# New places in the hand-laid order of a linear-attention and mixture-of-attention kernel: the first six chunks, the turning of x, and all the rest

## The chip, the cores and the metric

The kernel runs on one core of one Trainium2 chip. The metric is device time in microseconds (us), from the start of the program to its end. Time before: 364.91 us, the median of three runs (364.50 to 365.39).

## What is computed

Two layers, one behind the other, in float32.

```python
# layer 1, per batch b (4), head h (8), time t (768), head size 48
y[t]  = r[t] @ (state + outer(u * k[t], v[t]))
state = w[:, None] * state + outer(k[t], v[t])
# x = the heads of y side by side: 4 x 768 x 384
# layer 2, a mixture of 4 attentions; each token keeps its 2 best by the gate
logits = x @ w_gate
for e in range(4):
    q, k, v = x @ wq[e], x @ wk[e], x @ wv[e]          # 768 x 64 each
    a = softmax(causal(q @ k.T / 8))
    out += gate_weight[:, e:e+1] * (a @ v @ wo[e])      # weight 0 where e isn't kept
```

## The kernel before

**Chunks and groups.** Layer 1 runs in 24 chunks of 128 tokens (n = 0 to 23, six to a batch). Layer 2 runs in 8 groups of three chunks (G = 0 to 7, two to a batch): g = G % 2 is 0 for the first half of a batch and 1 for the second, which looks back at twice as many keys.

**A chunk** goes through these steps. `load_chunk` (L107, L108) and `load_vh` (L114) bring k, r and v by DMAs from the SP queue. `a_decay` (L279, L281) multiplies k and r by tables of powers of w, on VectorE (DVE) for the first three chunks and on GpSimd (POOL) after that. `a_ku` (L288, L290) runs on POOL. `a_transpose` turns k and r on TensorE (PE, L309), and ScalarE (ACT) copies them out (L315, L321). `a_state` (PE, L367) and `a_scores` (PE, L329) are issued together as a burst; `a_sum` (DVE, L378) and `a_put` (ACT, L388) take the state out, `a_mask` (two DVE instructions, L335) the scores. `a_out` (PE, L347) makes the outputs. `a_own` (two DVE instructions, L297 and L299) and `a_add` (DVE, L351) finish x, `a_clear` (POOL, L356) zeroes a buffer again. `a_xt` turns x on PE (L398) and copies the rounded high part out on ACT (L401); `a_xl` takes the low part on DVE (L408). For the first six chunks the second copies of v are not loaded again but copied on ACT (`load_zv`, four instructions at L128, and `copy_vh`, L119); later chunks load them by DMA (L130, L116).

**A group** goes through `m_proj` (keys and queries, PE L440; then ACT L450 and L455, DVE L452 and L457, and the DMA `tq<-xq` at L462), `m_values` (PE L473), `m_gate` (small DVE instructions), `m_scores` (PE L523 and L524, DVE L530, ACT L532), `m_weigh` (DVE L538 and L539, POOL L545), `m_turn` (PE L553, ACT L556), `m_av` (PE L570, ACT L576, DVE L577) and `m_out` (PE L586 to L588, ACT L590, store L592).

**Weights.** Each weight is loaded and split into a high and a low half: `load_qk`, `load_v`, `load_o` (SP), `hi_*` (ACT: L243, L256, L266), `lo_*` (DVE: L246, L259, L269).

**PSUM.** Every PE step but `m_scores` takes one of four buffers `ps`; `m_scores` takes one of two `psb`.

**What sets the order.** At the end of the kernel every step is put into a list with a place, a number in units of one group; the numbers in the dictionary `ORDER` are the offsets of the places. The list is sorted, and the steps are traced in that order. The framework's scheduler then lays each engine's queue by that order, and may let a step go ahead whose inputs its own time model holds ready while an earlier one is not; on the chip each queue runs strictly in the order laid. So a place is a priority, not a time. For a chunk the base is t = (n - 6) / 3 (plus `late` for chunks 3 to 5), and for a group's projection G - 1. Chunk n's burst stands at t + burst + slot[n % 6], its `a_out` just ahead of the burst of chunk n + 1.

Of the kernel before, what the change touches and what calls it, by code (L numbers as in the profile page):

```python
# [13 lines left out]
PSUM = bass.MemoryType.PSUM  # L14

ORDER = {
    "copy_vh": -0.4344, "xl": 0.0307, "own_step": 0.015, "add": 0.0416, "sum": 0.028, "mask": 0.1351, "clear":
    0.025, "weigh": 0.2685, "put": 0.2094, "load": -0.764, "decay": -0.4403, "late": 0.0203, "early": 0.1635,
    "early_project": -0.0474, "copy_zv": -0.5015, "load_uw": -0.4719, "load_vh": -0.5697, "load_zv": 0.0993,
    "transpose": -0.2131, "own": -0.3686, "burst": -0.0849, "xt": 0.376, "project": 0.1529, "project_step":  # L20
    0.0403, "attend": [-0.389, -0.3286], "av": [0.3013, 0.1265, 0.0118], "slot": [-0.0706, 0.0091, 0.0451,
    -0.0689, 0.0077, -0.0758], "mix": [0.4071, 0.6088], "mix_step": 0.0598, "load_qk": -0.8926, "load_v":
    0.3849, "load_o": 0.17, "attend_step": -0.0463, "values": 0.1812, "tail": 0.059, "tail_step": 1.2167,
}
FIRST = """
"""
# [12 lines left out]
def decay_attention_then_mixture_of_attention(  # L39
# [21 lines left out]
    NC = S // C  # L61
# [7 lines left out]
    GC = 3  # L69
# [203 lines left out]
    xt = {}  # L273
# [388 lines left out]
    def at(time, f, *args):  # L662
        steps.append((time, len(steps), f, args))

    for n in range(B * NC):
        t = (n - 2 * GC) / GC + (ORDER["late"] if GC <= n < 2 * GC else 0)
        at(t + ORDER["load"], load_chunk, n)
        at(t + ORDER["decay"], a_decay, n, 0)
        at(t + ORDER["decay"], a_decay, n, 1)
        at(t + ORDER["load_vh"], load_vh, n)  # L670
        at(t + ORDER["copy_zv" if n < EARLY_V else "load_zv"], load_zv, n)
        if n < EARLY_V:
            at(t + ORDER["copy_vh"], copy_vh, n)
        at(t + ORDER["transpose"], a_transpose, n)
        at(t + ORDER["own"], a_ku, n)

        at(t + ORDER["burst"] + 1 / GC + ORDER["slot"][(n + 1) % NC], a_out, n)
        at(t + ORDER["burst"] + 1 / GC + ORDER["slot"][(n + 1) % NC] + ORDER["own_step"], a_own, n)
        at(t + ORDER["burst"] + 1 / GC + ORDER["slot"][(n + 1) % NC] + ORDER["add"], a_add, n)
        if n + NL < B * NC:  # L680
            at(t + ORDER["burst"] + 1 / GC + ORDER["slot"][(n + 1) % NC] + ORDER["clear"], a_clear, n)
        t += ORDER["slot"][n % NC]
        at(t + ORDER["burst"] + 0.001, a_state, n)
        at(t + ORDER["burst"] + ORDER["sum"], a_sum, n)
        at(t + ORDER["burst"] + ORDER["put"], a_put, n)
        at(t + ORDER["burst"] + 0.003, a_scores, n)
        at(t + ORDER["burst"] + ORDER["mask"], a_mask, n)
        at(t + ORDER["xt"], a_xt, n)
        at(t + ORDER["xt"] + ORDER["xl"], a_xl, n)
    for G in range(NGR):  # L690
        g = G % NG
        nk = (g + 1) * GC
        t = G - 1 + ORDER["project"] - (0 if G else ORDER["early_project"])
# [6 lines left out]
        for e in range(E):  # L700
            t = G + e / E - (0 if G else ORDER["early"])
            if G == NGR - 1:
                t = G - ORDER["tail"] + e / E * ORDER["tail_step"]
# [88 lines left out]
```

## Time and profile before

| what | value |
|---|---|
| median of three runs | 364.91 us |
| the profiled execution's own time | 365.44 us |
| its span, first to last instruction | 363.7 us |
| busy in the span: PE, ACT, DVE, POOL | 94%, 72%, 63%, 54% |
| DMA, all 16 engines | 39.01 MB, mean 107 GB/s |

The profile is of one execution. Engines run at the same time; a share is busy time over the span. A wait in brackets, as `[1.20 <-DVE rabuf L335]`, is idle time of the engine just before the row and what ended it. Line numbers are those of the kernel before.

### The profile page before, as it was taken

How to read it: one execution, taken by the hardware profiler on the slowest of the kernel's cores; microseconds unless marked ns; L12 is line 12 of the kernel's file. 1: busy time of each engine (PE TensorE's matmuls, PEld its weight loads, DVE VectorE, ACT ScalarE, POOL GpSimd, SP SyncE). 2: the span in 40 equal slices, each digit the busy share in tenths (PEclk: the TensorE clock that was granted, in tenths of full speed). 3: DMA queues.
4: the chain of work that ended last, by engine and by line, in shares of the span. 5: the costliest groups of instructions: out<-in, count | busy, mean ns of one | idle time of the engine just before them, and what ended most of it. 6: DMA issues, size and time to landing. Idle time of an engine off the chain costs nothing.

```text
span 363.7 us, 10097 instructions
## 1 busy us (share of the span) xinstructions
PE 341.3 (94%) x3764; PEld 297.1 (82%) x3764; DVE 229.5 (63%) x645; ACT 261.2 (72%) x646; POOL 194.7 (54%) x272
## 2 busy tenths in 40 slices
PE   6877898999999999999999999999999999999995
PEld 2667787888899886999898896999898886998763
DVE  4897477778856565578667555478667554565400
ACT  7889667857885766757794857758795856778851
POOL 5389636856876267456776267465935053113520
PEclk9898999999999999999999999999999999999998
DMA  8994588484546945186637546196413410161101
GB/s 136 211 161 75 105 176 167 89 174 107 108 84 149 190 78 100 41 177 136 136 70 163 146 82 119 29 193 135 104 31 88 110 43 2 30 168 45 43 23 65
DMA packets 118484, 39.01 MB, mean 107 GB/s; under 512 B 111010, under 2 KB 114340, under 8 KB 118436
## 3 DMA queue, kind: packets, MB, share of 16 engines
q1 hardware_dynamic: 118436, 38.37, 52.0%
q8 instruction: 30, 0.49, 0.6%
q14 instruction: 18, 0.15, 0.1%
HBM read 21.05 MB, written 4.72 MB: 71 GB/s over the span
## 4 chain that ended last, share of the span: by engine, by line
PE 70%; DVE 9%; ACT 9%; DMA 4%; issue 4%; POOL 2%; SPq 1%; ACTq 0%; DVEq 0%; POOLq 0%
PE ps L440 11%; PE ps L570 11%; PE ps L553 8%; PE ps L473 7%; PE psb L523 5%; PE ps L347 5%; PE psb L524 5%; PE ps L309 5%; PE ps L586 3%; PE ps L367 2%; DMA tq<-xq 2%; PE ps L329 2%; PE ps L587 2%; PE ps L588 2%; DVE rabuf L335 2%
## 5 line engine op out<-in xcount | busy, mean ns | idle before, releaser
L545 POOL TENSOR_SCALAR pr<-pr,f,gate 128x128 f32<-128x128 f32 (+5 forms) x96 | 67.5, 716 | 84.0 <-DVE f L539 43.1
L530 DVE CUSTOM_DVE_ANT_0 pr<-psb,after 128x384 f32<-128x384 f32 (+5 forms) x96 | 58.8, 620 | 31.2 <-PE ps L553 20.0
L556 ACT ACTIVATE pt<-ps 128x384 f32<-128x384 f32 x144 | 55.7, 421 | 17.7 <-PE ps L553 15.7
L532 ACT ACTIVATE pr<-pr,nm 128x384 f32<-128x384 f32 (+5 forms) x96 | 64.2, 670 | 2.7 <-DVE nm L530 1.6
L553 PE MATMUL ps<-ident,pr 128*128 128x128 f32 x336 | 56.9, 278 | 1.2 <-ACT pt L556 0.9
L523 PE MATMUL psb<-tk,tq 128*128 128x384 f32 (+1 forms) x144 | 48.7, 341 | 3.8 <-DVE nm L530 2.3
L388 ACT ACTIVATE zvbuf<-z 64x384 f32<-64x384 f32 x48 | 25.1, 522 | 32.7 <-DVE z L378 28.3
L570 PE MATMUL ps<-pt,vv 128*64 128x384 f32 (+2 forms) x288 | 43.5, 422 | 0.3 <-ACT pt L556 0.3
L553 PEld LDWEIGHTS ps<-ident,pr 128*128 128x128 f32 x336 | 38.7, 141 | 6.0 <-ACT pt L556 1.8
L524 PE MATMUL psb<-tk,tq 128*128 128x384 f32 (+1 forms) x144 | 42.3, 312 | 0.0
L281 POOL TENSOR_TENSOR kdbuf<-kdbuf,tab_k 128x384 f32<-128x384 f32 x21 | 21.4, 1020 | 38.1 <-DMA kdbuf<-in_k_dram 29.9
L570 PEld LDWEIGHTS ps<-pt,vv 128*64 128x64 f32 x288 | 20.6, 137 | 20.9 <-issue 16.4
L335 DVE TENSOR_TENSOR rabuf<-ps,before 64x512 f32<-64x512 f32 x48 | 33.0, 688 | 1.9 <-PE ps L329 0.8
L440 PE MATMUL ps<-xt_hi,wqk_hi 128*128 128x384 f32 x96 | 33.9, 354 | 0.0
L440 PE MATMUL ps<-xt_hi,wqk_lo 128*128 128x384 f32 x96 | 32.3, 337 | 0.0
L440 PE MATMUL ps<-xt_lo,wqk_hi 128*128 128x384 f32 x96 | 32.3, 336 | 0.0
L523 PEld LDWEIGHTS psb<-tk,tq 128*128 128x128 f32 x144 | 27.2, 189 | 6.3 <-DVE nm L530 3.6
L347 PE MATMUL ps<-zvbuf,rabuf 128*64 128x48 f32 x768 | 29.6, 228 | 2.8 <-DVE rabuf L335 1.5
L347 PEld LDWEIGHTS ps<-zvbuf,rabuf 128*64 128x64 f32 x768 | 26.4, 141 | 6.7 <-ACT zvbuf L388 1.7
L329 PE MATMUL ps<-rabuf,kt 128*64 128x64 f32 x768 | 28.6, 224 | 1.5 <-DVE xq L457 1.0
L452 DVE TENSOR_TENSOR tk<-ps,tk 64x384 fp32r<-64x384 f32 x32 | 17.8, 555 | 19.3 <-ACT tk L450 18.6
L321 ACT ACTIVATE rabuf<-ps 64x512 f32<-64x512 f32 x48 | 28.2, 588 | 1.9 <-PE ps L309 1.6
(113 smaller groups left out, 782.8 us busy)
## 6 DMA issues: line engine op xcount, KB each, us to landing
tq<-xq SPq DMA_DIRECT2D x64, 192.0 KB, 3.5
kdbuf<-in_k_dram SPq DMA_DIRECT2D x24, 192.0 KB, 3.8
rdbuf<-in_r_dram SPq DMA_DIRECT2D x24, 192.0 KB, 3.6
vhbuf<-in_v_dram SPq DMA_DIRECT2D x24, 192.0 KB, 3.5
out_dram<-o SPq DMA_DIRECT2D x23, 192.0 KB, 2.0
zvbuf<-in_v_dram SPq DMA_DIRECT2D x72, 48.0 KB, 3.0
vhbuf<-in_v_dram SPq DMA_DIRECT2D x18, 96.0 KB, 3.3
pr<-in_moe_wk_dram SPq DMA_DIRECT2D x3, 128.0 KB, 3.9
```

Of the source, the lines that this page charges most:

```text
L329: nc.tensor.matmul(ps[rows, i, p, :], kt[:, p, half], ra[:, par, i, p, :], start=True, stop=True)
L335: nc.vector.tensor_tensor(ra[rows, par].rearrange("s i p t -> s (i p) t"), ps[rows].rearrange("s i p t -> s (i p) t"), before[rows, None, ...
L347: nc.tensor.matmul(ps[half, 2 * p + par, :], ra[:, par, i, p, :], zv[:, par, i, p, :], start=True, stop=True)
L440: nc.tensor.matmul(ps, a[:, t, m0:m0 + P], x[:, t, :], start=i == 0, stop=i == n - 1)
L523: nc.tensor.matmul(o, tq[e][:, 0, q], tk[:, e, :n], start=True, stop=False)
L524: nc.tensor.matmul(o, tq[e][:, 1, q], tk[:, e, :n], start=False, stop=True)
L530: nc.vector.tensor_tensor_reduce(pr[:, :N], ps, after[:, S - N:], 1.0, 3e38, op0=OP.add, op1=OP.min, accum_out=nm)
L532: nc.scalar.activation(pr[:, :N], pr[:, :N], AF.Exp, bias=nm, scale=-1.0, accum_out=sums[:, e, j, 0:1])
L545: nc.gpsimd.tensor_scalar(p[:, :N], p[:, :N], f[:, i], gate[:, i, e:e + 1], op0=OP.mult, op1=OP.mult)
L553: nc.tensor.transpose(pst[:, j, :], mg[G]["p", e, j][:, i * C:(i + 1) * C], ident)
L556: nc.scalar.activation(pt[:, j0:], pst[:, j0:], AF.Copy)
L570: nc.tensor.matmul(psy[par * HD:par * HD + HD, j0 * C:], vv[:, i % GC, e, :], mg[G]["t", e, i][:, j0:].rearrange("s j t -> s (j t)"), star ...
```

## The change

Five things are changed, all in the list of places; no instruction is added or removed. (1) Bursts of chunks 0 to 5 take their offset from a new list, `slot_first`; those of chunks 6 to 23 from `slot`. (2) `a_xt` and `a_xl` of chunk n are placed from the place of its `a_out` (by `xt_first` for chunks 0 to 5, by `xt` after that), and no longer from its burst. (3) `a_mask`, `a_sum`, `a_put`, `a_state`, `a_scores` keep their form. (4) All other numbers are new. (5) The rest of the code is rewritten to the same meaning.

```diff
 ORDER = {
-    "copy_vh": -0.4344, "xl": 0.0307, "own_step": 0.015, "add": 0.0416, "sum": 0.028, "mask": 0.1351, "clear":
-    0.025, "weigh": 0.2685, "put": 0.2094, "load": -0.764, "decay": -0.4403, "late": 0.0203, "early": 0.1635,
-    "early_project": -0.0474, "copy_zv": -0.5015, "load_uw": -0.4719, "load_vh": -0.5697, "load_zv": 0.0993,
-    "transpose": -0.2131, "own": -0.3686, "burst": -0.0849, "xt": 0.376, "project": 0.1529, "project_step":
-    0.0403, "attend": [-0.389, -0.3286], "av": [0.3013, 0.1265, 0.0118], "slot": [-0.0706, 0.0091, 0.0451,
-    -0.0689, 0.0077, -0.0758], "mix": [0.4071, 0.6088], "mix_step": 0.0598, "load_qk": -0.8926, "load_v":
-    0.3849, "load_o": 0.17, "attend_step": -0.0463, "values": 0.1812, "tail": 0.059, "tail_step": 1.2167,
+    "slot_first": [-0.0343, 0.0357, 0.066, -0.1135, -0.0011, -0.0651], "xt_first": 0.1508, "copy_vh": -0.3641,
+    "xl": 0.0089, "own_step": 0.0212, "add": 0.0461, "sum": 0.0171, "mask": 0.0441, "clear": 0.1139, "weigh":
+    0.347, "put": 0.1258, "load": -0.7169, "decay": -0.7152, "late": 0.0256, "early": 0.2341, "early_project":
+    -0.0171, "copy_zv": -0.4341, "load_uw": -0.4254, "load_vh": -0.4969, "load_zv": 0.0179, "transpose":
+    -0.2194, "own": -0.3837, "burst": -0.0773, "xt": 0.0468, "project": 0.1693, "project_step": 0.0363,
+    "attend": [-0.3869, -0.4547], "av": [0.3045, 0.1347, 0.0193], "slot": [0.0302, 0.0103, 0.0887, 0.012,
+    -0.0119, -0.0758], "mix": [0.4039, 0.5741], "mix_step": 0.0739, "load_qk": -0.8591, "load_v": 0.17,
+    "load_o": -0.0251, "attend_step": -0.0373, "values": 0.1807, "tail": 0.0527, "tail_step": 1.507,
 }
...
-        at(t + ORDER["burst"] + 1 / GC + ORDER["slot"][(n + 1) % NC], a_out, n)
...
-        t += ORDER["slot"][n % NC]
-        at(t + ORDER["burst"] + 0.001, a_state, n)
...
-        at(t + ORDER["xt"], a_xt, n)
-        at(t + ORDER["xt"] + ORDER["xl"], a_xl, n)
+        mine, next_one = (ORDER["slot_first"][x] if x < NC else ORDER["slot"][x % NC] for x in (n, n + 1))
+        t_out = t + ORDER["burst"] + 1 / GC + next_one
+        at(t_out, a_out, n)
...
+        at(t_out + ORDER["xt_first" if n < NC else "xt"], a_xt, n)
+        at(t_out + ORDER["xt_first" if n < NC else "xt"] + ORDER["xl"], a_xl, n)
+        t += ORDER["burst"] + mine
+        at(t + 0.001, a_state, n)
...
```

## Rows read from the trace of the kernel before

**Rows 1.** The page's first part: the span, then busy time, share and instructions of each engine.

```profile
span 363.7 us, 10097 instructions
PE 341.3 (94%) x3764; PEld 297.1 (82%) x3764; DVE 229.5 (63%) x645; ACT 261.2 (72%) x646; POOL 194.7 (54%) x272
```

**Rows 2.** Busy time of each engine by stage: the stretch in us, its length, then busy us (instructions) of PE, PE's weight loads, DVE, ACT, POOL, then PE's granted clock, the DMA share and GB/s.

```profile
0.00:9.50 9.50, 6.44 (x20) 2.47 (x20) 4.37 (x24) 7.12 (x13) 5.27 (x21) 1.00 0.85 139
9.50:37.00 27.50, 21.37 (x339) 18.77 (x339) 23.38 (x38) 24.44 (x54) 19.51 (x24) 0.88 0.95 145
37.00:50.00 13.00, 11.21 (x130) 10.46 (x130) 7.49 (x15) 7.28 (x17) 6.88 (x10) 1.00 0.72 141
50.00:100.00 50.00, 46.95 (x634) 42.59 (x632) 38.87 (x118) 36.83 (x93) 33.71 (x47) 1.00 0.66 131
100.00:345.00 245.00, 240.90 (x2559) 213.29 (x2561) 154.32 (x451) 178.84 (x455) 126.74 (x169) 1.00 0.46 100
345.00:364.00 19.00, 14.41 (x90) 9.53 (x86) 1.11 (x2) 6.71 (x18) 2.59 (x3) 0.93 0.11 42
```

**Rows 3.** The same for PE alone around the end of the third chunk: busy us, granted clock, DMA share, GB/s.

```profile
26.00:30.00 4.00, 2.02 (x31) 1.00 0.94 140
30.00:34.00 4.00, 3.21 (x54) 0.57 0.26 50
```

**Rows 4.** The chain of work that ended last, from 27 to 49 us: start, length, what.

```profile
27.25 0.34 DVE wv_lo L259
...
28.06 1.15 DVE wv_lo L259
...
29.24 0.69 DVE rabuf L335
...
29.97 0.69 DVE rabuf L335
...
41.16 0.49 ACT tk L450
...
42.25 0.57 DVE xq L457
...
43.43 4.93 DMA tq<-xq
```

**Rows 5.** PE in order of time at the start: start, length, what, and in brackets the idle time before it.

```profile
28.20 0.52 PE L398 MATMUL ps<-ident,ownv 128*128 128x128 f32 x3 [1.58 <-DVE ownv L351]
...
30.79 1.95 PE L347 MATMUL ps<-zvbuf,rabuf 128*64 128x48 f32 x32 [1.20 <-DVE rabuf L335]
...
40.07 1.14 PE L347 MATMUL ps<-zvbuf,rabuf 128*64 128x48 f32 x32
...
42.87 1.15 PE L329 MATMUL ps<-rabuf,kt 128*64 128x64 f32 x32 [0.98 <-DVE xq L457]
...
48.49 0.41 PE L523 MATMUL psb<-tk,tq 128*128 128x384 f32 x1 [0.81 <-DMA tq<-xq]
```

**Rows 6.** ACT in order of time, 39 to 41 us, same columns.

```profile
39.11 1.48 ACT L128 ACTIVATE zvbuf<-vhbuf 64x192 f32<-64x192 f32 x4 [1.16 <-DMA vhbuf<-in_v_dram]
40.61 0.52 ACT L119 ACTIVATE vhbuf<-vhbuf 64x384 f32<-64x384 f32 x1
```

**Rows 7.** The instructions of one line, `lo_v`: duration in ns, min/median/max, first and last start in us, form.

```profile
L259 DVE TENSOR_TENSOR wv_lo<-pr,wv_hi x3: 412/881/1231, 25.9 to 28.0; 128x260 fp32r<-128x260 f32 x3
```

**Rows 8.** Chunk 14 in the middle of the kernel, first PE and then DVE in order of time.

```profile
176.66 1.14 PE L347 MATMUL ps<-zvbuf,rabuf 128*64 128x48 f32 x32
177.63 0.85 PE L367 MATMUL ps<-vhbuf,kdbuf 128*64 128x96 f32 x16
178.31 1.10 PE L329 MATMUL ps<-rabuf,kt 128*64 128x64 f32 x32
179.34 0.44 PE L553 MATMUL ps<-ident,pr 128*128 128x128 f32 x2
179.53 0.42 PE L523 MATMUL psb<-tk,tq 128*128 128x384 f32 x1
...
179.48 0.55 DVE L351 TENSOR_TENSOR ownv<-ps,ownv 128x384 f32<-128x384 f32 x1
180.06 1.39 DVE L335 TENSOR_TENSOR rabuf<-ps,before 64x512 f32<-64x512 f32 x2
```

**Rows 9.** Who waited for whom over the whole span: us in total, times, longest.

```profile
POOL pr L545 <- DVE f L539: 43.1, 12, 12.7
POOL kdbuf L281 <- DMA kdbuf<-in_k_dram: 29.9, 9, 4.6
PE ps L398 <- DVE ownv L351: 2.3, 3, 1.6
```

**Rows 10.** The tail: PE and then POOL in order of time.

```profile
341.83 0.34 PE L523 MATMUL psb<-tk,tq 128*128 128x384 f32 x1
342.00 0.34 PE L524 MATMUL psb<-tk,tq 128*128 128x384 f32 x1
...
342.58 3.44 PE L570 MATMUL ps<-pt,vv 128*64 128x384 f32 x22
347.56 3.82 PE L553 MATMUL ps<-ident,pr 128*128 128x128 f32 x30
...
345.05 2.59 POOL L545 TENSOR_SCALAR pr<-pr,f,gate 128x512 f32<-128x512 f32 x3 [3.29 <-DVE f L539]
```

More of the change, by code (lines that the diff above doesn't have):

```diff
@@ L675, in decay_attention_then_mixture_of_attention @@
         at(t + ORDER["own"], a_ku, n)
-        at(t + ORDER["burst"] + 1 / GC + ORDER["slot"][(n + 1) % NC], a_out, n)
-        at(t + ORDER["burst"] + 1 / GC + ORDER["slot"][(n + 1) % NC] + ORDER["own_step"], a_own, n)
-        at(t + ORDER["burst"] + 1 / GC + ORDER["slot"][(n + 1) % NC] + ORDER["add"], a_add, n)
-        if n + NL < B * NC:
-            at(t + ORDER["burst"] + 1 / GC + ORDER["slot"][(n + 1) % NC] + ORDER["clear"], a_clear, n)
-        t += ORDER["slot"][n % NC]
-        at(t + ORDER["burst"] + 0.001, a_state, n)
[L684 to L687, printed above, removed]
-        at(t + ORDER["xt"], a_xt, n)
-        at(t + ORDER["xt"] + ORDER["xl"], a_xl, n)
+        mine, next_one = (ORDER["slot_first"][x] if x < NC else ORDER["slot"][x % NC] for x in (n, n + 1))
+        t_out = t + ORDER["burst"] + 1 / GC + next_one
+        at(t_out, a_out, n)
+        at(t_out + ORDER["own_step"], a_own, n)
+        at(t_out + ORDER["add"], a_add, n)
+        if n + NL < B * NC:
+            at(t_out + ORDER["clear"], a_clear, n)
+        at(t_out + ORDER["xt_first" if n < NC else "xt"], a_xt, n)
+        at(t_out + ORDER["xt_first" if n < NC else "xt"] + ORDER["xl"], a_xl, n)
+        t += ORDER["burst"] + mine
+        at(t + 0.001, a_state, n)
+        at(t + ORDER["sum"], a_sum, n)
+        at(t + ORDER["put"], a_put, n)
+        at(t + 0.003, a_scores, n)
+        at(t + ORDER["mask"], a_mask, n)
     for G in range(NGR):
```

## The prediction

> **What bounds the kernel now.** I read the page's busy shares first: PE is busy 94% of 363.7 us, no other engine over 72% [rows 1]. A share is a mean over stages, so the table by stage comes next [rows 2]. From 100 to 345 us PE is busy 240.9 of 245 us: there the kernel is PE's queue, run without pause, and a new order of the same work can give back 4.1 us at most. The idle time lies ahead of that: 3.1 us from 0 to 9.5 (first loads, which the change hardly touches), 6.1 from 9.5 to 37, 1.8 from 37 to 50, 3.05 from 50 to 100; and 4.6 in the tail, most of it the last copy and store. From 9.5 to 37 DVE (23.4 of 27.5) and ACT (24.4) are fuller than PE (21.4): that stretch is a chain that hops between them. The chain of work that ended last [rows 4] shows where: DVE's split of the gate and value weights stands ahead of the masks of chunk 2, and behind them PE's `a_out`. Last I read PE's own waits in order of time [rows 5]: 1.58 us before x of chunk 1 is turned, 1.20 before `a_out` of chunk 2, 0.98 before a `a_scores` and 0.81 before the first `m_scores`.
>
> The profiled execution took 365.44 us, 1.74 more than its span. The sum is made against 365.44; the median shown, 364.91, is 0.53 lower, and that is taken off at the end.
>
> **The change, part by part.** No instruction is added or removed, so a price is always that of a wait that goes or comes.
>
> (1) *37 to 50 us: ACT's order at the first projection.* The places before: `load_zv` of chunk 5 at -0.8145, `m_proj(0,1,0)` at -0.7997, `copy_vh` of chunk 5 at -0.7474. So ACT took the four copies of v first, waited 1.16 us for their DMA, and spent 1.48 and 0.52 us on them [rows 6]; only at 41.16 could it copy the keys out, and DVE the queries at 42.25 [rows 4]. PE's next burst needed a PSUM buffer of that projection and stood 0.98 us; the queries' DMA landed late, and `m_scores` stood 0.81 us [rows 5]. After: `m_proj(0,1,0)` -0.8136, `m_proj(0,0,0)` -0.7773, `load_zv` -0.7418, `copy_vh` -0.6718. The projection goes first, and the copies, 2.0 us, move behind it. Both waits are shorter than that, so I take both: **-1.8** (bounds -1.8 and 0, if the scheduler still holds the copies ready first). Late next is the second copy of v for chunk 5, which its burst and `a_out` need more than 10 us on.
>
> (2) *9.5 to 37 us: the chain of the first three chunks.* `load_v` with its splits moves from -1.6151 to -1.83, ahead of `a_out` of chunk 0; `load_o` from -1.83 to -2.0251. `a_mask` moves ahead of `a_add` (chunk 2's mask -1.3005, chunk 1's add -1.2985; before -1.238 and -1.3315). The last split, 1.15 us, stands between that add and the masks [rows 4]; without it `a_out` of chunk 2 loses its 1.20 wait. But the split isn't gone, it stands earlier, on an engine that is 85% busy there. Bounds: -2.78, both waits of [rows 5]; and +1.4, two masks of 0.69 put ahead of an add that PE waits for. I take **-1.0**, nearer to what one wait gives, since the busy time of DVE and ACT stays. One form of the split took 0.41 to 1.23 us [rows 7].
> The Trainium skill (SBUF — State Buffer, section Who interferes with whom) has a rule on that: a VectorE instruction with two inputs in SBUF and a GpSimd instruction that reads SBUF shut each other out until the first is done. The rows agree in size: the longest of the three is three times the shortest at the same form. By that rule the term would hang on what POOL does at the split's new place, which is the fourth case below.
>
> (3) *50 to 100 us.* Bursts of chunks 6 and 7 move (0.108 later, 0.001 later), the second group's `m_scores` come 0.126 earlier, `early` shifts the first group's attention forward by 0.07. PE idles 3.05 us here in short waits that each have another cause. The rows exclude neither sign: bounds -3.05 and +3.05. I take **-0.6**, a fifth, because this stretch gets offsets of its own for the first time.
>
> (4) *100 to 345 us: x turned right behind its outputs.* Before, `a_xt` stood 0.376 behind its burst's place, which put it 0.05 to 0.24 behind `a_out`; now always 0.0468. Chunk 14 shows what that means [rows 8]: PE starts `a_out` at 176.66, has state and scores issued by 179.34, and one turn and one `m_scores` take 0.79 more, so by place it would reach `a_xt` 3.47 us after the start. `a_add` ended at 180.03, 3.37 us after it. That fits, barely. But the masks (1.39 us) now stand ahead of the add (0.0441 against 0.0461). In all, PE waited for an add 3 times, 2.3 us, all before 70 us [rows 9]. Bounds: 0, and 1.4 for each chunk that has only short steps behind its burst (places 1, 2 and 4 of six, three batches): +12.6. I take **+0.6**, three chunks at 0.2, nearest to the trace, where no later chunk waited: the scheduler lets PE go on with a turn while x isn't ready.
>
> (5) *POOL and SP.* `a_decay` moves from 0.32 to 0.002 behind its load. POOL already waits for these loads, 29.9 us in nine waits [rows 9]; it is 54% busy, and what queues behind is `m_weigh`, for which POOL itself idles 43.1 us. So 0; if that cover went, a weighing (2.59 us [rows 10]) would come late and PE's turns with it. `load_chunk` 0.047 later, `load_zv` 0.08 and `a_put` 0.08 earlier, `a_clear` 0.09 later, `m_weigh` 0.08 later: each lies beside PE's backlog: 0. The loads of `load_v`, three large DMAs and three tiny ones, move on SP ahead of chunk 3's, which wait behind them; chunk 3 is turned only behind the bursts of chunks 0 to 2, which cover that: 0.
>
> (6) *The tail.* `tail_step` grows, `m_out` of group 6 goes ahead. By place the last two `m_scores` now fall behind `m_av(7,0)`. I take 0, since the scheduler let these `m_scores` go ahead of their place before; the price otherwise is a case below.
>
> Sum: -1.8 - 1.0 - 0.6 + 0.6 = -2.8; 365.44 - 2.8 = 362.64, less 0.53: **362.1 us**. Terms (2) and (3) are shares of idle time, the least certain of it.
>
> **The rivals.**
> *More is regained* (chance 0.11). All waits named go: 1.8, 2.78 and 3.05, and with the gap before `a_out` of chunk 2 the fall of the clock: PE was busy 2.02 of 4 us, then had 0.57 of its clock [rows 3], between its levels of 1.2 and 2.4 GHz, and `a_out` took 1.95 us instead of 1.14 [rows 5], 0.8 more. 8.4 us: 356.5. Against it: DVE and ACT have only 3 to 4 us free there.
>
> *Slower: x waits behind the masks* (0.27). Place: chunks 6 to 23. Price: with both masks ahead, the add ends 3.37 + 1.39 us after `a_out` starts and PE can turn x 0.15 later, at 4.9; it reaches the place at 3.47 in place 2 (wait 1.4), and in places 1 and 4, where an `m_out` of six matmuls at 0.17 [rows 10] lies between as well, at 4.5 (wait 0.4 to 0.5). Per batch 2.3, three batches 6.9; with the 3.4 gained at the start, 364.91 - 3.4 + 6.9 = 368.4. It decides from a mean of 0.2 us per chunk on. For it: 0.15 us after the add is where PE started at the waits of [rows 5]. Against: the scheduler fills PE.
>
> *The tail opens* (0.05). From the last `m_scores` (done by 342.5) to its weights' end on POOL (347.64) are 5.1 us, covered by `m_av` and `m_out` [rows 10]; with these ahead, only six turns, half of 3.82 us, are left: +3.2, so 365.3.
>
> *No change* (0.11). The places are priorities only; the scheduler lays the start much as before, or DVE's splits meet POOL's earlier decays and take 1.23 each (3 x 1.23 - 2.52 = 1.2 more, and the same for the two of `load_o`), which eats terms (2) and (3) and half of (1): 364.9. By the rule of the Trainium skill named above (SBUF — State Buffer, Who interferes with whom) this is what earlier decays on POOL would do.
>
> **How the numbers follow.** Forecast 0.46, own range 359.4 to 364.0 (terms 1 to 3 at four fifths of their joint bound of 7.6 us, or at a fifth). The second, third and fourth rival end at 368.4, 365.3, 364.9. About 0.2%, 0.73 us, is what can be told from no change. Faster: 0.46 + 0.11 = 0.57; same: 0.05 + 0.11 = 0.16; slower 0.27. The range leaves out half of the first rival and about two fifths of the second: 356.8 to 368.4.
>
> **What would show it.** Step 1: ACT's first key copy near 38.5 instead of 41.16, and no PE wait before the fifth burst. Step 2: DVE done with the value split before the masks of chunk 1 or 2, the first projection before 36.66. Step 4: PE's waits for the add in total: under 4 us right, over 8 wrong. Step 6: no PE gap between the last two `m_turn` groups. Wrong altogether: PE's idle time from 100 to 345 us over 8 us, or the start as long as before.

## The result, and the profile after

The changed kernel is slower: 367.99 us (366.25 to 372.4, 10 runs) against 365.10 (363.18 to 365.97, 10 runs) for the kernel before. The ratio is 1.0086, 95% interval 1.0061 to 1.0111; it leaves out the two longest runs, 372.25 and 372.4 us. Forecast were 362.1 us and a gain. The profiled execution after is the one of 372.25 us; another profiled one of the same kernel, `e_again` below, took 365.38, the shortest of all. So verdicts go by the ratios over many runs, and the traces are read for what they have in common. Line numbers are one higher than before.

The page's first part, and then busy time by stage with the columns of [rows 2]:

```profile
span 370.5 us, 10092 instructions
PE 346.1 (93%) x3764; PEld 301.2 (81%) x3764; DVE 232.8 (63%) x645; ACT 261.4 (71%) x646; POOL 194.5 (52%) x272
```

```profile
0.00:9.50 9.50, 6.31 (x20) 2.47 (x20) 5.13 (x23) 6.85 (x12) 5.00 (x21) 1.00 0.91 138
9.50:37.00 27.50, 18.89 (x289) 16.54 (x290) 22.36 (x32) 21.33 (x47) 15.49 (x20) 0.82 0.88 140
37.00:50.00 13.00, 10.76 (x162) 9.95 (x158) 8.31 (x16) 9.26 (x21) 9.26 (x12) 0.98 0.48 102
50.00:100.00 50.00, 47.62 (x554) 44.24 (x555) 35.60 (x113) 34.21 (x88) 29.75 (x43) 0.93 0.62 126
100.00:345.00 245.00, 241.38 (x2620) 213.41 (x2618) 156.90 (x452) 177.20 (x448) 129.56 (x173) 1.00 0.48 102
```

Against [rows 1, 2]: from 100 to 345 us PE idles 3.6 us now and 4.1 before. From 9.5 to 37 it idles 8.6 instead of 6.1, at a granted clock of 0.82 instead of 0.88. By its first matrix product each projection starts as follows: the first at 40.39 (before 36.66), the second at 74.05 (67.57), the last at 316.79 (310.09). From the second to the last it takes 242.7 us now and 242.5 before. In this execution the whole loss lies ahead of 74 us: 3.7 us of it at the first projection, and 2.75 more between the first and the second, where the granted clock was 0.83 from 50 to 60 us (before 1.00). In `e_again` the stretch between the two is only 0.65 us longer than before, so most of the 2.75 belongs to this one execution. PE in order of time there, against [rows 5]:

```profile
22.39 0.52 PE L399 MATMUL ps<-ident,ownv 128*128 128x128 f32 x3 [1.23 <-DVE ownv L352]
...
25.11 1.14 PE L348 MATMUL ps<-zvbuf,rabuf 128*64 128x48 f32 x32 [1.33 <-DVE rabuf L336]
...
32.05 0.87 PE L399 MATMUL ps<-ident,ownv 128*128 128x128 f32 x3 [3.77 <-DVE ownv L352]
...
34.56 1.95 PE L348 MATMUL ps<-zvbuf,rabuf 128*64 128x48 f32 x32
...
50.15 0.41 PE L524 MATMUL psb<-tk,tq 128*128 128x384 f32 x1 [2.04 <-DMA tq<-xq]
```

The wait of 1.20 us ahead of `a_out` of chunk 2 is gone, as forecast. The wait for x of chunk 1 grew from 1.58 to 3.77, and x of chunk 0 and `a_out` of chunk 1 now wait as well, 1.23 and 1.33 us (in `e_again` 0.17 and 0.30). Behind the longest wait the granted clock was 0.59 from 30 to 34 us, between its levels of 1.2 and 2.4 GHz, and `a_out` of chunk 2 took 1.95 us where that of chunk 1 had taken 1.14; before, it was much the same, 0.57 and 1.95 [rows 3, 5]. The first `m_scores` waited 2.04 us for the queries' DMA, before 0.81. What PE waits for at 32.05 stands on DVE; DVE and then POOL in order of time:

```profile
25.70 0.41 DVE L260 TENSOR_TENSOR wv_lo<-pr,wv_hi 128x260 fp32r<-128x260 f32 x1
26.34 0.56 DVE L298 TENSOR_REDUCE ps<-ku 128x8 f32<-128x384 f32 x1 [0.24 <-issue]
26.89 3.61 DVE L260 TENSOR_TENSOR wv_lo<-pr,wv_hi 128x260 fp32r<-128x260 f32 x1
30.43 0.54 DVE L300 TENSOR_TENSOR ownv<-vhbuf,ps 128x384 f32<-128x384 f32 x1
30.89 0.54 DVE L379 TENSOR_TENSOR z<-ps,z 128x384 f32<-128x384 f32 x1
31.36 0.54 DVE L352 TENSOR_TENSOR ownv<-ps,ownv 128x384 f32<-128x384 f32 x1
```

```profile
26.25 1.09 POOL L357 MEMSET rabuf<- 64x512 f32 x2 [3.14 <-PE ps L348]
27.31 1.00 POOL L282 TENSOR_TENSOR rdbuf<-rdbuf,tab_r 128x384 f32<-128x384 f32 x1
28.28 0.98 POOL L289 TENSOR_TENSOR ku<-kdbuf,uw 128x384 f32<-128x384 f32 x1
29.23 0.98 POOL L282 TENSOR_TENSOR kdbuf<-kdbuf,tab_k 128x384 f32<-128x384 f32 x1
31.58 0.51 POOL L384 TENSOR_TENSOR z<-z,w 128x192 f32<-128x192 f32 x1 [1.37 <-DVE z L379]
```

The third split of the value weights took 3.61 us; at the same size the second took 0.41. It ended at 30.50, 0.29 us after the last of three GpSimd instructions in a row that read SBUF (29.23 + 0.98 = 30.21), and only when GpSimd had to pause for DVE's sum. Behind it on DVE's queue stood the weighing with v, the sum and the addition of chunk 1, so x of chunk 1 was late. Before, the three splits took 2.52 us together [rows 7]. The last of them, 1.23 us from 27.98 on, ran beside these two GpSimd instructions, and ended at 29.21, 0.29 us after the first of the two:

```profile
27.92 1.00 POOL L281 TENSOR_TENSOR kdbuf<-kdbuf,tab_k 128x384 f32<-128x384 f32 x1
28.88 1.19 POOL L290 TENSOR_TENSOR ku<-ku,rdbuf 128x384 f32<-128x384 f32 x1
```

ACT at the first projection, against [rows 6], and two rows of who waited for whom, against [rows 9]:

```profile
42.50 1.49 ACT L129 ACTIVATE zvbuf<-vhbuf 64x192 f32<-64x192 f32 x4 [0.82 <-DMA vhbuf<-in_v_dram]
44.00 0.53 ACT L120 ACTIVATE vhbuf<-vhbuf 64x384 f32<-64x384 f32 x1
44.55 0.48 ACT L451 ACTIVATE tk<-ps 64x384 fp32r<-64x384 f32 x1
```

```profile
POOL kdbuf L282 <- DMA kdbuf<-in_k_dram: 38.8, 14, 4.6
...
PE ps L399 <- DVE ownv L352: 6.0, 4, 3.8
```

ACT still copies chunk 5's v ahead of the first keys, whatever the places say. PE waits 6.0 us for an addition in all, 3.8 of it at chunk 1, and all of it ahead of 73 us.

### The profile page after: what moved, and what is told of

It reads as the page before. It is cut to its first block, busy times and chain, and to the rows that moved or that the text cites. A ratio compares the mean times of both kernels' runs of the same rounds, so it can differ in the third digit from the quotient of the medians.

```text
span 370.5 us, 10092 instructions
## 1 busy us (share of the span) xinstructions
PE 346.1 (93%) x3764; PEld 301.2 (81%) x3764; DVE 232.8 (63%) x645; ACT 261.4 (71%) x646; POOL 194.5 (52%) x272
## 4 chain that ended last, share of the span: by engine, by line
PE 77%; DVE 9%; ACT 5%; issue 3%; DMA 3%; SPq 2%; ACTq 0%; DVEq 0%
PE ps L441 12%; PE ps L571 11%; PE ps L554 9%; PE ps L474 7%; PE psb L524 6%; PE ps L348 6%; PE psb L525 5%; PE ps L310 4%; PE ps L330 4%; PE ps L368 3%; PE ps L587 2%; PE ps L588 2%; PE ps L589 2%; DVE rabuf L336 2%; PE ps L399 2%
## 5 line engine op out<-in xcount | busy, mean ns | idle before, releaser
L524 PE MATMUL psb<-tk,tq 128*128 128x384 f32 (+1 forms) x144 | 49.3, 345 | 3.6 <-DMA tq<-xq 2.0
L525 PE MATMUL psb<-tk,tq 128*128 128x384 f32 (+1 forms) x144 | 42.7, 314 | 0.0
L441 PE MATMUL ps<-xt_lo,wqk_hi 128*128 128x384 f32 x96 | 33.5, 349 | 0.0
L441 PE MATMUL ps<-xt_hi,wqk_lo 128*128 128x384 f32 x96 | 33.4, 348 | 0.0
```

The lines of the kernel that those rows point to most:

```text
L441: nc.tensor.matmul(ps, a[:, t, m0:m0 + P], x[:, t, :], start=i == 0, stop=i == n - 1)
L524: nc.tensor.matmul(o, tq[e][:, 0, q], tk[:, e, :n], start=True, stop=False)
L525: nc.tensor.matmul(o, tq[e][:, 1, q], tk[:, e, :n], start=False, stop=True)
```

## The experiments

Each kernel was timed 4 to 12 times (4 for `e_start_new` and `e_lov_late`) beside runs of the kernel before, whose median was 364.62 to 365.18 us. The two durations are those of each kernel's own profiled execution: the longest of the three splits, and PE's longest wait for an addition.

| kernel | longest split, ns | longest wait, us | median, us | ratio to before, 95% |
|---|---|---|---|---|
| before | 1231 | 1.6 | | 1 |
| `e_again` | 3266 | 2.7 | 367.74 | 1.0088 (1.0058 to 1.0119) |
| `e_start_old` | 1242 | 1.7 | 365.56 | 1.0009 (0.9990 to 1.0028) |
| `e_start_new` | 3436 | 2.9 | 369.60 | 1.0118 (1.0059 to 1.0178) |
| `e_lov_pool` | 742 (GpSimd) | 3.2 | 367.82 | 1.0080 (1.0053 to 1.0107) |
| `e_splits_old` | 1568 | 2.3 | 365.62 | 1.0026 (0.9996 to 1.0056) |
| `e_splits_new` | 3339 | 2.8 | 367.80 | 1.0086 (1.0048 to 1.0125) |
| `e_lov_one` | (275, a fill) | 1.0 | 364.53 | 0.9993 (0.9970 to 1.0016) |
| `e_lov_psum` | 426 | 1.2 | 365.27 | 1.0012 (0.9983 to 1.0041) |
| `e_lov_late` | 4569 | 1.2 | 370.37 | 1.0156 (1.0112 to 1.0201) |
| `e_lov_xl` | 3296 | 1.2 | 364.12 | 0.9988 (0.9964 to 1.0011) |
| `e_both_xl` | 2684 | 0.8 | 364.89 | 1.0005 (0.9981 to 1.0030) |
| `e_both_xl_b` | 1250 | 0.4 | 364.19 | 0.9973 (0.9948 to 0.9999) |

**Which part of the change.** `e_again` is the changed kernel once more. `e_start_old` has the old places for the start and the new ones for the rest; `e_start_new` is its mirror image.

```diff
+    def order_of(first):          # e_start_old; e_start_new the other way round
+        return OLD if (True if first else False) else NEW
     for n in range(B * NC):
+        PL = order_of(n < NC)
...
-        at(t + ORDER["load"], load_chunk, n)
+        at(t + PL["load"], load_chunk, n)
```

> The changed kernel as it is, for a second trace. Theory A (the lock): VectorE's third split of the value weights is shut out by three GpSimd instructions in a row and takes over 2.5 us again (3.61 in the first trace), PE waits over 3 us for x of chunk 1, the first projection starts after 39.5 us, and the time is 367 to 369. Theory B (the rest of the order): that long split belongs to one execution; here it is under 1.5 us and the time is near 368 all the same.

> Old places for chunks 0 to 5, group 0 and the loads of weights; new places for all the rest. A: the loss is all in the start, so 364 to 365.5, a ratio to before of 0.997 to 1.002, first projection near 36.7 us. B: the new places of chunks 6 to 23 (x right behind its outputs) carry the loss: 367 to 369.

> The reverse: new places for chunks 0 to 5, group 0 and the loads of weights; old places for the rest. A: 367 to 369, as the whole change, with the first projection after 39.5 us. B: 364 to 366.

The slowdown repeats, the new start alone has all of it, and the new places of the rest make no difference that can be measured. `e_again` missed two of its smaller signs: PE waited 2.7 us for x of chunk 1, not over 3, and the first projection came at 37.79 us, not after 39.5.

The start has two halves: the weights' loads with their splits, and the places of the chunks' own steps. `e_splits_old` and `e_splits_new` exchange the first half alone.

```diff
-    ... "load_v": 0.17, "load_o": -0.0251      e_splits_old: the changed kernel
+    ... "load_v": 0.3849, "load_o": 0.17       e_splits_new: the reverse, in the kernel before
```

> The changed kernel with one pair of places put back: the loads and splits of the value and output weights (load_v 0.3849, load_o 0.17, as before the change). Theory A, the place of these splits and of their loads is the cause: the third split of the value weights (L260) takes at most 1.3 us instead of 3.3 to 3.6, TensorE waits for x of chunk 1 under 1 us, the first projection starts before 38 us, and the time is that of the kernel before, 364.5 to 366. Rival D, the new places of the first six chunks (masks ahead of additions, x right behind its outputs) are the cause: the time stays at 367 to 368.5.

> The kernel before with one pair of places new: load_v 0.17 and load_o -0.0251, nothing else of the change. Its TensorE order is that of the kernel before to the last instruction. Theory A: VectorE's and GpSimd's order at 20 to 35 us become those of the changed kernel, the third split takes over 2.5 us, TensorE waits 2 us or more for x of chunk 1, the first projection starts after 38.5 us and the time is 367 to 369. Rival D: 364.5 to 366, with the split in 1.3 us.

Two numbers carry it, as far as can be measured: `load_v` and `load_o`. Put new into the kernel before, without a change on PE's queue, they cost 0.86%; taken out of the changed kernel they leave 0.26% with an interval that takes in 1 (0.9996 to 1.0056), so that a smaller share of the other new places of the start is not excluded. Two of the smaller signs of `e_splits_old` missed: a split of 1.57 us (it ended 0.3 us after the one GpSimd instruction beside it) and a wait of 2.3 were more than expected. Its first projection came at 37.53, as expected.

**What makes the split long.** `e_lov_pool` moves the three splits to GpSimd. `e_lov_one` leaves them out and fills their place with zeros. `e_lov_psum` leaves every queue as it is and reads the second input from an old tile in PSUM, so that the low halves hold other numbers.

```diff
-        nc.vector.tensor_tensor(wv_lo[:, t, :], raws["v", t][:, :NV + E], wv_hi[...], op=OP.subtract)
+        nc.gpsimd.tensor_tensor(wv_lo[:, t, :], raws["v", t][:, :NV + E], wv_hi[...], ...)          # e_lov_pool
+        nc.vector.memset(wv_lo[:, t, :].bitcast(F32), 0.0)                                          # e_lov_one
+        nc.vector.tensor_tensor(wv_lo[:, t, :], wv_hi[...], tables["ps"][:, 0]..., op=OP.subtract)  # e_lov_psum
```

> The changed kernel with the three splits of the value weights (lo_v) computed on GpSimd instead of VectorE, all places as they are. A: with nothing on VectorE to be shut out, PE's wait before x of chunk 1 falls from 3.77 us to under 1.5, the first projection starts at 36.5 to 38.5, and the time is 364 to 366. Rival C: GpSimd gets three instructions of 0.7 us more ahead of chunk 3's decay, so the wait moves to the turning of chunk 3 and the time stays at 367 to 369.

> The changed kernel without the three splits of the value weights: their low halves are filled with zeros at the very start, so what they add to the values is left out. The orders of TensorE, ScalarE and SyncE are those of the changed kernel, GpSimd's too but for one pair. Theory B, the split that is held up by GpSimd is the whole of it: TensorE waits under 0.7 us for x of chunks 1 and 2 each, the first projection starts before 37.7 us, the time is 364 to 365.5. Rival C, GpSimd itself is the late one in this stretch (as with the splits moved to it): the wait moves to x of chunk 2, which stands over 1.5 us behind products that come late, and the time stays at 366.5 to 368.

> The changed kernel with another second input for the three splits of the value weights: they subtract an old tile in PSUM from the high half in SBUF, so the low halves hold other numbers. The orders of all five queues are those of the changed kernel to the last instruction; the splits keep their size, their place and what they wait for, and read one input from SBUF instead of two. Theory B (two SBUF inputs on VectorE are shut out while GpSimd runs instructions that read SBUF): all three splits take under 0.6 us with GpSimd as busy beside them as before, TensorE waits under 0.7 us for x of chunk 1, and the time is that without the splits, 364 to 365.5. Rival F (it is the place of the splits in VectorE's order, or something else that comes with it, and the long duration is only where a wait is shown): the third still takes over 2 us and the time stays at 367 to 368.5.

`e_lov_pool`, in which the scheduler also laid a few instructions of the other queues differently, gained nothing: x of chunk 1 no longer waited, but GpSimd, with 2.2 us more to do, was late with the products of chunk 2, and x of chunk 2 waited 3.2 us. Without the splits (`e_lov_one`) all of the loss was back, and no wait moved on, so GpSimd's own lateness was an effect of that edit, not of the change. `e_lov_psum` settles the mechanism. Its splits, and GpSimd beside them:

```profile
L260 DVE TENSOR_TENSOR wv_lo<-wv_hi,psb x3: 413/414/426, 24.2 to 26.0; 128x260 fp32r<-128x260 f32 x3
```

```profile
25.26 1.09 POOL L357 MEMSET rabuf<- 64x512 f32 x2 [1.61 <-PE ps L348]
26.33 1.01 POOL L282 TENSOR_TENSOR rdbuf<-rdbuf,tab_r 128x384 f32<-128x384 f32 x1
27.30 1.00 POOL L289 TENSOR_TENSOR ku<-kdbuf,uw 128x384 f32<-128x384 f32 x1
```

The same instruction at the same place, with the same GpSimd instructions behind the same fill, took 0.41 us where it had taken 3.27 to 3.61 with both inputs in SBUF. It began 0.30 us ahead of the first GpSimd instruction that reads SBUF (26.03 and 26.33); the long ones, in four traces, 0.07 to 0.42 ahead. The three VectorE instructions behind it, each with at most one input in SBUF, took 0.55 us each beside the same GpSimd run. PE at the start of `e_lov_psum`, the waits of some length:

```profile
22.22 0.52 PE L399 MATMUL ps<-ident,ownv 128*128 128x128 f32 x3 [1.22 <-DVE ownv L352]
24.13 1.14 PE L348 MATMUL ps<-zvbuf,rabuf 128*64 128x48 f32 x32 [0.52 <-DVE rabuf L336]
...
29.70 1.14 PE L348 MATMUL ps<-zvbuf,rabuf 128*64 128x48 f32 x32 [0.24 <-DVE rabuf L336]
```

x of chunk 1, between the last two, did not wait. The Trainium skill (SBUF — State Buffer, section Who interferes with whom) names exactly this pair, a VectorE instruction with two SBUF inputs and a GpSimd instruction that reads SBUF, and this trace agrees. Its section SBUF: two separate sides says too that whichever of the two starts first has the pair of ports for its whole instruction. By the start times in the trace of the changed kernel that does not come out: the 3.61 us split began at 26.89, the first GpSimd instruction that reads SBUF at 27.31.

**Can the splits be put out of the way?** Three kernels hold them back on DVE by an order of its queue: `e_lov_late` behind the addition of chunk 2, `e_lov_xl` behind the low half of x of chunk 2, `e_both_xl` there with the splits of the output weights too; `e_both_xl_b` is that in the kernel before.

```diff
-        nc.vector.tensor_tensor(wv_lo[:, t, :], raws["v", t][:, :NV + E], wv_hi[...], op=OP.subtract)
+        split = nc.vector.tensor_tensor(wv_lo[:, t, :], raws["v", t][:, :NV + E], wv_hi[...], op=OP.subtract)
+        tc.add_manual_dep(split.ins, st["xl", 2].ins.name, in_queue, reason="late")   # e_lov_late: st["added", 2]
```

> The changed kernel with the three splits of the value weights held back behind the addition of chunk 2 on VectorE (some 35 us) by an order of the queue; nothing else is edited. Theory B: nothing is held up ahead of x of chunks 1 and 2, and behind it the splits lie in front of the masks of chunk 3, which no matrix product of the first projection waits for: 364 to 365.5, first projection before 37.8 us. Rival C: 366.5 to 368, with the wait at x of chunk 2. Rival E, the splits only delay other work there (the low half of x of chunk 2, the masks of chunk 3): the first projection after 38.5 us or a wait of over 1.5 us for a mask behind it, 366 to 368.

> The changed kernel with the three splits of the value weights held back behind the low half of x of chunk 2 on VectorE, where it had no work from 37.9 to 42 us in the runs without them. The splits may be held up there too, for up to 4 us, as they were behind the addition of chunk 2 (4.57 us), but what stands behind them (the key halves of the first projection, some 5 us after its start) is not yet due. Theory B: 364 to 365.5, first projection before 37.8 us, no wait of TensorE over 1 us for the key halves or the values. Rival E: they end after 43 us and hold up the key halves and the query halves, 366 to 368.

> As the kernel before this one in the list, with the two splits of the output weights held back to the same place. In the changed kernel these stand around the addition of chunk 0 and ahead of the masks of chunk 1, which x of chunk 0 and the outputs of chunk 1 waited for (1.23 and 1.33 us in its trace). Theory B: some 1 us more is regained, 363 to 365. Rival E: VectorE now has 2.3 us of splits and what holds them up ahead of the key halves, 366 to 368.

> The kernel before with all five splits held back in the same way, all places old. In its trace they took 2.5 us for the value weights (412, 881 and 1231 ns) and up to 2.4 us for the output weights, part of it ahead of the addition and the masks of chunk 1. Theory B: 362.5 to 364.5, faster than before by 0.1 to 0.6 per cent. Rival C (the old order hides the splits): within 0.2 per cent of before. Rival E: slower, 366 or more.

`e_lov_late` missed, and was the slowest of all. Its splits, GpSimd beside them, and PE behind:

```profile
L260 DVE TENSOR_TENSOR wv_lo<-pr,wv_hi x3: 417/1064/4569, 35.2 to 40.6; 128x260 fp32r<-128x260 f32 x3
```

```profile
35.87 0.71 POOL L384 TENSOR_TENSOR z<-z,w 128x192 f32<-128x192 f32 x1
36.54 0.99 POOL L282 TENSOR_TENSOR kdbuf<-kdbuf,tab_k 128x384 f32<-128x384 f32 x1
37.49 1.00 POOL L282 TENSOR_TENSOR rdbuf<-rdbuf,tab_r 128x384 f32<-128x384 f32 x1
38.46 0.99 POOL L291 TENSOR_TENSOR ku<-ku,rdbuf 128x384 f32<-128x384 f32 x1
39.41 1.01 POOL L282 TENSOR_TENSOR kdbuf<-kdbuf,tab_k 128x384 f32<-128x384 f32 x1
```

```profile
42.54 0.69 PE L441 MATMUL ps<-xt_hi,wqk_hi 128*128 128x384 f32 x1 [4.45 <-DVE rabuf L336]
```

The second split began at 36.14 and ended at 40.71, again 0.29 us after GpSimd's run ended (39.41 + 1.01). Behind it stood the masks, for which the projection had to stop, 4.45 us by the row's releaser, and the low half of x of chunk 2 came only behind them. `e_lov_xl` has a split of 3.30 us as well, but nothing due stands behind it, and it runs as fast as the kernel without the splits. So the length of the split costs nothing that can be measured by itself; what is queued behind it decides. `e_both_xl` did not bring its further microsecond. In the kernel before, the same edit (`e_both_xl_b`) gives 364.19 us, 0.27% less; its interval leaves out 1, but by 0.0001 only, and as one of twelve versions that shows no gain for certain.

## Why the prediction was wrong

It was wrong in step (2) first of all, and in step (1). Step (2) saw that the splits only move, on an engine that is 85% busy, and took -1.0 us, from the wait that goes, with +1.4 as the worst. It looked for what the splits would be late for, and not for what would run beside them at the new place. There the third met three GpSimd instructions. `e_splits_new` sizes the whole of this step's move of the loads at +0.86%, some 3.1 us of 365. The mechanism stood in the text, as part of the case of no change with a chance of 0.11, but priced at "1.23 each": the split was taken to lose to one GpSimd instruction, as in [rows 7]; in four traces with the new places it lost to every one of a run of three and took 3.27 to 3.61. Between the forecast of -2.8 us and the loss of 2.9 lie 5.7; step (2), at +3.1 in place of -1.0, makes up about 4.1 of them, and step (1), at 0 in place of -1.8, another 1.8, which is about all.

The wait that step (2) wanted gone did go: the 1.20 us ahead of `a_out` of chunk 2 went to 0.24 in `e_lov_psum`. But with the long split taken away, the change as a whole is 1.0012 (0.9983 to 1.0041): no difference. In that trace the output weights' splits, moved ahead of the addition of chunk 0, gave x of chunk 0 a new wait of 1.22 us (1.23 in the changed kernel). That this is what used up the gain is not shown: in `e_both_xl` the wait of x of chunk 0 is gone too, and it is at 1.0005 (0.9981 to 1.0030). In `e_lov_xl` and `e_lov_one` the first projection starts 2.0 and 2.1 us earlier than before (34.68 and 34.57, at a granted clock of 1.00 from 9.5 to 37 us), the second only 0.4 and 0.9 (67.21 and 66.64): most of what is gained at the start is gone by the second projection, and why stays open.

Step (1), -1.8 us, did not happen. ACT's first key copy comes at 44.55, 4.16 us after the projection's start, against 4.50 before, and the copies of chunk 5's v still stand ahead of it. The 0.98 us ahead of the burst's `a_scores` are gone, but the first `m_scores` waits 2.04 for the queries' DMA: 2.04 in all against 1.79 before. The bound of 0, the copies staying ahead, was the right end.

Step (3), -0.6, and step (4), +0.6: `e_start_old` has both, but for the shift of the first group's attention, and is at 1.0009 (0.9990 to 1.0028), so their sum cannot be told from 0; neither was tried alone. (Step (3) has a slip: by the numbers of the change the bursts of chunk 7 move 0.009 later, not 0.001; its price does not hang on that.) Past 100 us PE idles 3.6 us, under the 8 that would have shown x waiting behind masks: that rival, which had the right sign, had the wrong place, and that its 368.4 us lies so near the measured 367.99 is luck.

Step (5), 0, holds. With the decays' old place put back into the changed kernel the scheduler lays all five queues the same, instruction by instruction, so that place does nothing. The loads of `load_v` ahead of chunk 3's were costed at 0 on SP; the queue they mattered on was DVE's. Step (6), 0, holds: from the last projection's start to PE's last instruction it is 49.5 us against 49.4.

**The size in one execution.** `e_again`'s profiled execution has the long split, a wait of 2.7 us and its first projection 1.1 us later than before, and yet its span is 363.7 us, that of the kernel before. PE idled 0.8 us less than before from 50 to 100 us and 0.6 less from 100 to 345. Its clock was 0.94 of full from 9.5 to 37 us, against 0.88 before and 0.82 in the changed kernel's first profile. Why the clock falls more in one execution than in another was not tried and stays open. Ten runs of `e_again` spread over 4.9 us, so a single profile of each kernel cannot size this change.

## What to carry over

Before moving an instruction with two SBUF inputs on VectorE, read GpSimd's timeline at the new place: put its worst price at the whole uninterrupted run of GpSimd instructions there, not at one of them, and then see what is queued behind it. If such an instruction has to run beside a busy GpSimd, put it where nothing due follows (`e_lov_xl`), or give it one input from PSUM (`e_lov_psum`). And a place in a priority list is not an order: look whether the queue changes at all before giving a move a price.

## What the runs showed of the hardware

A VectorE instruction with both inputs in SBUF, 0.41 us long by itself, took as long as 4.57 us beside GpSimd instructions of about 1 us each in a row, and every split of the value weights that lost to a run ended 0.29 to 0.30 us after the run's last instruction. In other cases a split came in after the first GpSimd instruction (it ended at 29.21 in the kernel before [rows 4], and the GpSimd instruction behind it then took 1.19 us; that line's mean is 1.01). What decides between the two was not found. A GpSimd fill, whose row names no input, did not hold one up: in `e_splits_new` the second split took 0.42 us beside one.
